# Eighty-four idle transposes ahead of each layer of experts, and two scatters moved behind the counts

## The chip, the cores and the metric

The kernel runs on one core of one Trainium2 chip. The metric is the device time of one execution in microseconds (us); lower is better. A profiled execution was taken by the hardware profiler beside the timed runs. [...] "Cold" below means 0.50, "warm" 1.00.

## The reference

Attention that keeps the 32 largest scores of each row, and then two layers of experts on the 2304 rows of its output. Each row goes to the one expert (of eight) with the highest logit.

```
scores = q @ k.T / 8 ; all but the top 32 of a row are masked ; attn = softmax(scores) @ v
x  = rows of attn                                          # 2304 x 512
# first layer
e  = argmax(x @ w_gate) ; p = softmax(x @ w_gate)[e]
x  = p * (relu(x @ w1[e]) @ w2[e])                          # w1 512x1024, w2 1024x512
# second layer, only for rows with x @ w_skip > 0; the others stay as they are
out = x + p * (relu(x @ w1[e]) @ w2[e])
```

## The kernel before

All matrix products are done in float32 (the products of the experts as three float32r products of a high and a low part). The program has three stages.

The **attention** takes the first 530 us. Each finished tile of 128 rows is gated at once: the expert of each row is picked, its place in that expert's list is counted, and GpSimd (POOL) scatters the row with an indirect DMA into a table in DRAM, `rows[0]`, which is sorted by expert.

The **first layer** of experts (`Moe.layer(0, ...)`, experts g = 0 to 7) reads blocks of 128 rows of one expert after the other. The **second layer** (g = 8 to 15) does the same from `rows[1]`. For one expert, in `Moe.expert`: `xT` transposes each block of rows on TensorE (line 690), ScalarE copies the high part out of PSUM (L692) and VectorE takes the low part (L693); `mm1` makes the hidden units, eight groups of twelve matmuls (L706), whose width (192 to 512 columns) is chosen by the count of rows; `mm2` makes the output, 24 matmuls of 512 columns a block (L730). The first two blocks (j = 0 and 1) are always computed, the others only where the expert has that many rows. The weights come in pieces by DMA into `raw` buffers, and are split into high and low parts by ScalarE (L653) and by GpSimd or VectorE (L655), next to the matmuls.

After each block of the first layer, `FirstPost` gates its rows for the second layer, and its step `places` ends with two scatters on GpSimd's queue (L541): one of the row into `rows[1]`, and one of the row into the kernel's output, which is the final value of a row that skips the second layer. The block is kept meanwhile in one of six buffers `yo`, which `slot(g, j)` picks; expert 7 has its blocks 0 and 1 in `yo2` and `yo3`.

A layer begins in `Moe.layer`: SyncE loads the first blocks of rows (L662, `xg<-x`), which must wait for the scatters into the same table; all engines read the first count of rows into a register (`counts(0)`, L669 and L670); then the experts follow. Between the layers stands a conditional part for experts with more rows than the blocks hold (L803); it isn't entered here, but where its two ways meet GpSimd waits for its own outstanding scatters and then sets their semaphores (`INC_SWDGE_SEM` in the rows) to the count that the other way would have left. A similar conditional part (L1002) stands between attention and the first layer.

At the start of the program the kernel already has idle transposes of the identity matrix, twenty and then six at a time (`keep_warm`, L150), into a PSUM tile that nobody reads.

Of the kernel before, what the change touches and what calls it, by code (L numbers as in the profile page):

```python
# [8 lines left out]
F32 = mybir.dt.float32  # L9
# [467 lines left out]
HF = 5  # L477
D0 = 1
F0 = (0, 1, 2, 3)
LO = ((1, 3, 5, 7), (1, 3, 5))  # L480


# [10 lines left out]
def top_expert(tc, ev, lg, f, ob, mask=None):  # L493


    nc = tc.nc

    def first():
        nc.vector.scalar_tensor_tensor(f[:, 8:16], lg, f[:, 0:1], ev.rev8, op0=OP.is_ge, op1=OP.mult)

    def onehot():
        if mask is None:
            one_port(tc, ev, ob, f[:, 8:16], f[:, 2:3], OP.is_equal)
        else:
            nc.vector.tensor_scalar(ob, f[:, 8:16], f[:, 2:3], mask, op0=OP.is_equal, op1=OP.mult)

    return [lambda: nc.vector.tensor_reduce(out=f[:, 0:1], in_=lg, op=OP.max, axis=AX.X),
            lambda: nc.vector.tensor_scalar(f[:, 1:2], f[:, 0:1], -1.0, None, op0=OP.mult),
            first,
            lambda: nc.vector.tensor_reduce(out=f[:, 2:3], in_=f[:, 8:16], op=OP.max, axis=AX.X),  # L510
            onehot]


def take_place(tc, ev, sb, base, f, ob, r=None):

    nc = tc.nc
    at = []

    def ranks():
        p = ev.ps.tile([128, 2, 8], F32, name="m", bufs=ev.mb)  # L520
        nc.tensor.matmul(p[:, 0], ev.tri, ob, start=True, stop=True)
        nc.tensor.matmul(p[:, 1], ev.ones, ob, start=True, stop=True)
        if r is not None:
            nc.scalar.activation(r, p, AF.Copy)
        at.append(p if r is None else r)

    def move():
        p = at.pop()
        nc.vector.tensor_tensor(f[:, 16:24], p[:, 0], base, op=OP.add)
        nc.vector.tensor_tensor(base, p[:, 1], base, op=OP.add)  # L530

    def pick():
        nc.vector.scalar_tensor_tensor(f[:, 24:32], f[:, 16:24], 1.0, ob, op0=OP.mult, op1=OP.mult,
                                       accum_out=f[:, 3:4])

    return [ranks, move, pick]


def scatter(tc, ev, dst, idx, src, group=None):

    w = tc.nc.gpsimd.indirect_dma_start(out=dst, out_offset=bass.IndirectOffsetOnAxis(ap=idx, axis=0), in_=src,  # L541
                                        in_offset=None, bounds_check=dst.shape[0] - 1, oob_is_err=False)
    if group:
        tc.declare_no_dep(w.ins, group=group, reason="every token has its own row")
        tc.add_to_no_dep_group(group, w.ins)
    return w
# [51 lines left out]
class Moe:  # L598
# [4 lines left out]
    def __init__(self, tc, ev, pool, weights):  # L603
        self.tc, self.ev, self.ws = tc, ev, weights
        self.W1 = [pool.tile([128, 2, 1024], F32R, name="w1_%d" % i) for i in range(4)]
        self.RAW = [pool.tile([128, 1024], F32, name="raw%d" % i) for i in range(3)]
# [26 lines left out]
    def fetch(self, k):  # L633

        if k >= 128:
            return
        layer, e = divmod(k // 8, 8)
        w1, w2 = self.ws[layer]
        raw, c = self.raw(k), k % 8
        if c < 4:  # L640
            self.tc.nc.sync.dma_start(raw, w1[e, c * 128:(c + 1) * 128, :])
        else:
            self.tc.nc.sync.dma_start(raw.rearrange("p (a d) -> p a d", a=2),
                                      w2[e, (c - 4) * 256:(c - 3) * 256, :].rearrange("(a p) d -> p a d", p=128))
# [13 lines left out]
    def load(self, g, j):  # L658
        layer, e = divmod(g, 8)
        rows = self.ev.rows[layer]  # L660
        r0 = e * (rows.shape[0] // 8) + j * 128
        self.tc.nc.sync.dma_start(self.XG[g % 2][j], rows[r0:r0 + 128])  # L662
# [79 lines left out]
    def expert(self, g):  # L742


        layer, e = divmod(g, 8)
        post, nxt = self.posts[layer], e < 7
        for j in range(2):
# [10 lines left out]
        for f in range(8):  # L758
            self.mm1(g, f)
            for i in range(4):  # L760
                if F0[i] == f:
                    self.split(8 * g + 4 + i, post.lo)
# [27 lines left out]
    def layer(self, layer, ns):  # L790
        tc, nc = self.tc, self.tc.nc
        g0 = layer * 8
        self.ns, self.n, self.open_rows = ns, {}, []
        for j in range(BLOCKS[layer]):
            self.load(g0, j)
        self.counts(0)
        if layer == 0:
            for k in range(6, 3 + NR):
                self.fetch(k)
        for e in range(8):  # L800
            self.expert(g0 + e)
        most = nc.values_load(ns[0:1, 8:9], min_val=0, max_val=18)  # L802
        with tc.If(most > BLOCKS[layer]):  # L803
            self.rest(layer, ns)
# [55 lines left out]
def slot(g, j):  # L860
    return j + 2 if j > 1 else 2 * (g % 2) + j


class FirstPost:

    lo = LO[0]

    def __init__(self, tc, ev, mo, wgt, out):
        Dm = out.shape[1]
        self.tc, self.ev, self.out, self.wgt = tc, ev, out, wgt  # L870
        self.yo = [mo.tile([128, Dm + 2], F32, name="yo%d" % i) for i in range(6)]
        self.ix = [mo.tile([128, 2], I32, name="ix%d" % i) for i in range(6)]
        self.fx = [mo.tile([128, 48], F32, name="fx%d" % i) for i in range(6)]
        self.ob = [mo.tile([128, 8], BF, name="ob%d" % i) for i in range(6)]
        self.yT = [mo.tile([128, 4, 128], F32, name="yT%d" % i) for i in range(2)]
        self.rk = [mo.tile([128, 2, 8], F32, name="rk%d" % i) for i in range(6)]
        self.ex = mo.tile([128, 8], F32, name="ex")
        self.D = Dm

    def __call__(self, g, j, xg, p):  # L880
# [4 lines left out]
    def later(self, g, j):  # L885
        tc, nc, ev, D = self.tc, self.tc.nc, self.ev, self.D
        i = slot(g, j)
        y, ix, f, ob, yT = self.yo[i], self.ix[i], self.fx[i], self.ob[i], self.yT[j % 2]
        lg, sk, tok = f[:, 32:40], f[:, 40:41], y[:, D + 1:D + 2]

        def nop():
            pass

        def turn():
            p = ev.ps.tile([128, 4, 128], F32, name="m", bufs=ev.mb)
            for c in range(4):
                nc.tensor.transpose(p[:, c], y[:, c * 128:c * 128 + 128], ev.ident)
            nc.scalar.activation(yT, p, AF.Copy)

        def logits():  # L900
            p = ev.ps.tile([128, 9], F32, name="m", bufs=ev.mb)
            for c in range(4):
                nc.tensor.matmul(p, yT[:, c], self.wgt[:, c], start=(c == 0), stop=(c == 3))
            nc.vector.tensor_copy(f[:, 32:41], p)
            a[0]()
            nc.vector.tensor_scalar(f[:, 41:42], sk, 0.0, None, op0=OP.is_gt)
            a[1]()
            a[2]()
            nc.vector.tensor_scalar(f[:, 42:43], sk, 0.0, OOB, op0=OP.is_le, op1=OP.mult)
            a[3]()  # L910
            nc.scalar.activation(self.ex, lg, AF.Exp, bias=f[:, 1:2], accum_out=f[:, 4:5])
            nc.vector.scalar_tensor_tensor(ix[:, 1:2], f[:, 41:42], OOB, tok, op0=OP.mult, op1=OP.add)
            a[4]()

        def places():
            b[0]()
            nc.vector.tensor_scalar(f[:, 5:6], f[:, 4:5], 1e-9, None, op0=OP.add)
            b[1]()
            nc.vector.reciprocal(y[:, D:D + 1], f[:, 5:6])
            b[2]()  # L920
            nc.vector.tensor_scalar(ix[:, 0:1], f[:, 3:4], f[:, 42:43], None, op0=OP.add)
            scatter(tc, ev, ev.rows[1], ix[:, 0:1], y, ev.moe_groups[0])
            scatter(tc, self.ev, self.out, ix[:, 1:2], y[:, :D], ev.moe_groups[1])

        a = top_expert(tc, ev, lg, f, ob, f[:, 41:42])
        b = take_place(tc, ev, None, ev.base[1], f, ob, self.rk[i])
        return [turn, nop, logits, nop, nop, places]


class SecondPost:  # L930
    lo = LO[1]

# [132 lines left out]
```

## Time and profile before

| | |
|---|---|
| timed runs | 1097.92, 1098.09 and 1105.02 us; median 1098.09 |
| profiled execution, its own time | 1106.61 us |
| its span, first to last instruction | 1104.8 us |
| what lies around the span | 1.8 us |
| granted TensorE clock, mean | 0.914 of full |

The profiled execution is 8.5 us above the median of the runs. Two of the three timed runs are within 0.2 us of one another, the third is 7 us above them. Times inside the profile are counted from the span's start: attention to about 530 us, the first layer to about 865 us, the second to the end.

### The profile page before, as it was taken

The page shows a single profiled execution, that of the slowest core. Times are in us where ns is not written, and L with a number is a line of the kernel's source. Part 1 is how long each engine was busy: PE and PEld are TensorE (multiplying, and loading weights), DVE is VectorE, ACT ScalarE, POOL GpSimd, SP SyncE. Part 2 cuts the span into 40 slices and gives each one's busy share as a digit, 9 for nine tenths or more (in the row PEclk, how much of TensorE's full clock was granted, in tenths as well). Part 3 has the DMA queues.
Part 4 walks back from the last instruction along what each step waited for, and adds up shares of the span by engine and source line. Part 5 has one row for each costly group of instructions (what it writes and reads, how often), then busy time and mean ns, then how long its engine had stood idle before and what let it go on. Part 6 is the DMA issues. An engine that isn't in the chain of part 4 may idle for free. (4 is left out here: it accounts for less than half of the span.)

```text
span 1104.8 us, 20918 instructions
## 1 busy us (share of the span) xinstructions
PE 915.3 (83%) x6389; PEld 725.8 (66%) x6389; DVE 780.9 (71%) x3483; ACT 687.6 (62%) x1420; POOL 621.1 (56%) x451
## 2 busy tenths in 40 slices
PE   7577777787977778789499899988999499999994
PEld 5345554555655455457488778867877398898884
DVE  7999999999899999997226456446635256644441
ACT  5689999997879989975235435435543154443340
POOL 3777887787587978842224344334324266665461
PEclk9689999998888889989599899988999599999998
DMA  9991010101102000001635454456425367665530
GB/s 302 297 265 65 1 65 2 65 2 53 51 33 99 22 20 20 1 2 40 222 116 174 129 151 146 141 167 191 145 88 154 101 187 219 218 211 168 177 103 14
DMA packets 55051, 127.90 MB, mean 116 GB/s; under 512 B 8105, under 2 KB 8105, under 8 KB 54864
## 3 DMA queue, kind: packets, MB, share of 16 engines
q1 hardware_dynamic: 48464, 112.89, 33.1%
q0 software_dynamic: 6400, 12.65, 3.1%
q8 instruction: 101, 1.65, 0.6%
q14 instruction: 86, 0.70, 0.2%
HBM read 96.04 MB, written 37.86 MB: 121 GB/s over the span
## 5 line engine op out<-in xcount | busy, mean ns | idle before, releaser
L655 POOL TENSOR_TENSOR w<-raw,w 128x1024 fp32r<-128x1024 f32 x74 | 179.5, 2435 | 219.4 <-ACT w L653 143.2
L730 PE MATMUL y<-w,h 128*128 128x512 f32 x960 | 240.2, 404 | 10.5 <-ACTq L679 5.0
L212 POOL TENSOR_TENSOR y<-s,sg 128x576 f32<-128x576 f32 x144 | 203.9, 1438 | 64.4 <-ACT sg L209 48.3
L706 PE MATMUL hp<-xT,w 128*128 128x192 f32 (+4 forms) x1536 | 221.1, 302 | 10.7 <-DVE h L721 6.7
L706 PEld LDWEIGHTS hp<-xT,w 128*128 128x128 f32 x1536 | 209.9, 195 | 16.5 <-DVE h L721 8.7
L730 PEld LDWEIGHTS y<-w,h 128*128 128x128 f32 x960 | 181.1, 193 | 54.8 <-issue 10.3
L181 DVE MAX8 ca<-s 128x8 f32<-128x82 f32 (+1 forms) x1008 | 159.3, 228 | 6.1 <-ACT s L170 6.1
L295 PE MATMUL m<-ident,p 128*128 128x128 f32 x576 | 98.0, 298 | 74.4 <-DVE x L326 52.3
L259 POOL TENSOR_TENSOR r<-s,r 128x576 f32<-128x576 f32 x96 | 137.5, 1447 | 28.9 <-DVE r L255 18.4
L295 PEld LDWEIGHTS m<-ident,p 128*128 128x128 f32 x576 | 66.8, 149 | 116.1 <-ACT p L267 31.1
L721 DVE SCALAR_TENSOR_TENSOR h<-hp,h 128x512 fp32r<-128x512 f32 (+1 forms) x128 | 77.8, 621 | 82.6 <-ACT h L720 82.1
L653 ACT ACTIVATE w<-raw 128x1024 fp32r<-128x1024 f32 x128 | 133.6, 1055 | 0.5 <-ACTq L679 0.5
L720 ACT ACTIVATE h<-hp 128x512 fp32r<-128x512 f32 (+1 forms) x128 | 68.3, 543 | 75.2 <-PE hp L706 72.1
L209 ACT ACTIVATE sg<-s,tm 128x576 f32<-128x576 f32 x144 | 111.5, 792 | 5.6 <-POOL tm L200 5.6
L655 DVE TENSOR_TENSOR w<-raw,w 128x1024 fp32r<-128x1024 f32 x54 | 86.9, 1609 | 37.2 <-ACTq L679 27.2
L219 DVE MAX8 my<-y 128x8 f32<-128x576 f32 x144 | 101.9, 746 | 1.9 <-POOL y L212 1.9
L124 PE MATMUL m<-pT,v 128*64 128x128 f32 (+1 forms) x1280 | 95.2, 298 | 8.2 <-ACT pT L301 7.0
L97 PE MATMUL s<-kT,qT 64*128 64x288 f32 x512 | 90.5, 475 | 12.5 <-ACT s L170 12.5
L170 ACT ACTIVATE s<-s 128x1152 f32<-128x1152 f32 (+1 forms) x73 | 81.9, 1123 | 18.8 <-PE s L97 16.2
L301 ACT ACTIVATE pT<-m 128x512 f32<-128x512 f32 x137 | 78.5, 609 | 23.8 <-PE m L295 23.6
L124 PEld LDWEIGHTS m<-pT,v 128*64 128x64 f32 x1280 | 75.3, 155 | 21.4 <-ACT pT L301 11.5
L267 ACT ACTIVATE p<-r,neg 128x576 f32<-128x576 f32 x96 | 74.7, 784 | 3.4 <-POOL r L259 3.2
(133 smaller groups left out, 1302.1 us busy)
## 6 DMA issues: line engine op xcount, KB each, us to landing
raw<-in_moe_w_dram SPq DMA_DIRECT2D x128, 512.0 KB, 4.4
x<-zrow SPq DMA_DIRECT2D x16, 1028.0 KB, 19.2
xg<-x SPq DMA_DIRECT2D x56, 257.0 KB, 3.7
v<-in_v_dram SPq DMA_DIRECT2D x8, 576.0 KB, 4.2
kT<-in_k_dram SPq DMA_DIRECT2D x7, 576.0 KB, 4.4
qT<-in_q_dram SPq DMA_DIRECT2D x7, 576.0 KB, 5.8
out_dram<-yo,ix POOLq DMA_INDIRECT x40, 4.8
kT<-in_k_dram SPq DMA_DIRECT2D x2, 288.0 KB, 3.8
```

The lines of the kernel that those rows point to most:

```text
L97: nc.tensor.matmul(p[:, c, :288], d["qT"][h, b, t * 128:t * 128 + 128], d["kT"][h, b, cs], start=True, stop=True)
L124: nc.tensor.matmul(po[i * 64:i * 64 + 64, cs], d["vt"][:, b, i, c] if c < 4 else d["v8"][i * 64:i * 64 + 64, b], pts[i][:, c, cs] if c < 4 ...
L181: nc.vector.max(out=ca[:, c], in_=e["s"][hh][:, cut[c]:cut[c + 1]])
L209: nc.scalar.activation(sg, e["s"][hh], AF.Sign, bias=bt["tm"][:, w:w + 1], scale=-ONE_BELOW, accum_out=bt["ac"][:, w:w + 1])
L212: nc.gpsimd.tensor_mul(y, e["s"][hh], sg)
L219: nc.vector.max(out=bt["my"][:, 2 * i + hh, 8:], in_=e["y"][hh])
L259: nc.gpsimd.tensor_tensor(r, e["s"][hh], r, op=OP.subtract)
L295: nc.tensor.transpose(pp[:, c], e["p"][:, hh, c * 128:c * 128 + 128], ident)
L653: nc.scalar.activation(t[:, 0], raw, AF.Copy)
L655: eng.tensor_tensor(t[:, 1], raw, t[:, 0].bitcast(F32), op=OP.subtract)
L706: nc.tensor.matmul(p[:, :W], self.w1(g, c)[:, a, fs], x[:, c, b, :W], start=(i == 0), stop=(i == 11))
L730: nc.tensor.matmul(p, self.HT[f][:, a, js], self.W2[f // 2][:, b, f % 2 * 512:f % 2 * 512 + 512], start=(f + a + b == 0), stop=(f == 7 and ...
```

## The change

Two things. In `Moe.layer`, behind the loads of the first rows and the first count, 84 transposes of the identity into a fresh tile `m` of PSUM that nobody reads; so in both layers. And the scatters to the output of blocks 0 and 1 of the first layer's last expert (g = 7) are kept back in a list, and are issued at the beginning of the second layer, behind its `counts(0)`.

```diff
+WARM2 = 84
@@ Moe.layer
         for j in range(BLOCKS[layer]):
             self.load(g0, j)
         self.counts(0)
+        for fn in self.posts[0].skipped:
+            fn()
+        self.posts[0].skipped = []
+        p = self.psum.tile([128, 4, 128], F32, name="m", bufs=self.ev.mb)
+        for i in range(WARM2):
+            nc.tensor.transpose(p[:, i % 4], self.ev.ident, self.ev.ident)
         if layer == 0:
@@ FirstPost.__init__
+        self.skipped = []
@@ FirstPost.later, places()
             scatter(tc, ev, ev.rows[1], ix[:, 0:1], y, ev.moe_groups[0])
-            scatter(tc, self.ev, self.out, ix[:, 1:2], y[:, :D], ev.moe_groups[1])
+            self.skipped.append(lambda: scatter(tc, ev, self.out, ix[:, 1:2], y[:, :D], ev.moe_groups[1]))
+            if g % 8 < 7 or j > 1:
+                self.skipped.pop()()
```

TensorE at the beginning of the first layer, before. `ns` holds the counts, `m` is a tile of PSUM, `xg` a block of rows, `ident` the identity:

```order
L1002 UNCONDITIONAL_BRANCH x2
L669 TENSOR_LOAD ns
L670 TENSOR_LOAD ns
L690 MATMUL m<-ident,xg_10121 128x128 x4
L690 MATMUL m<-ident,xg_10122 128x128 x4
L679 COMPARE_AND_BRANCH x2
L690 MATMUL m<-ident,xg_10124 128x128 x4
L679 UNCONDITIONAL_BRANCH x2
L690 MATMUL m<-ident,xg_10123 128x128 x4
```

The same place after the change (the numbers of the lines are a little higher in the changed file):

```order
L670 TENSOR_LOAD ns
L671 TENSOR_LOAD ns
L803 MATMUL m<-ident 128x128 x84
L691 MATMUL m<-ident,xg_10121 128x128 x4
L691 MATMUL m<-ident,xg_10122 128x128 x4
L680 COMPARE_AND_BRANCH x2
L691 MATMUL m<-ident,xg_10124 128x128 x4
```

The 84 transposes stand between the reading of the counts and the first transposes of rows; nothing else moved on TensorE. At the beginning of the second layer the same 84 stand behind the same two loads of `ns`.

GpSimd at the end of the first layer, before. `yo3` and `yo2` are blocks 1 and 0 of its last expert, `x1` is the table `rows[1]`, `out_0_dram` the output, and L802 and L803 begin the conditional part between the layers:

```order
L541 DMA x1_83<-yo3_10086,ix3_10092 18432x514
L541 DMA out_0_dram<-yo3_10086,ix3_10092 2304x512
L541 DMA x1_83<-yo2_10085,ix2_10091 18432x514
L541 DMA out_0_dram<-yo2_10085,ix2_10091 2304x512
L802 TENSOR_LOAD ns_10157
L803 COMPARE_AND_BRANCH
```

The same place after the change:

```order
L542 DMA x1_83<-yo3_10086,ix3_10092 18432x514
L542 DMA x1_83<-yo2_10085,ix2_10091 18432x514
L809 TENSOR_LOAD ns_10157
L810 COMPARE_AND_BRANCH
```

Only the two scatters to the table are left there. GpSimd after the change where the second layer begins; `ns_17471` holds its counts:

```order
L810 ISA
L810 UNCONDITIONAL_BRANCH
L670 TENSOR_LOAD ns_17471
L542 DMA out_0_dram<-yo3_10086,ix3_10092 2304x512
L542 DMA out_0_dram<-yo2_10085,ix2_10091 2304x512
L680 COMPARE_AND_BRANCH
```

The two scatters to the output moved from between and behind those to the table to the far side of the place where the conditional part ends, and of the reading of the count. The wait for outstanding scatters and `INC_SWDGE_SEM` (the `ISA` row) now stand ahead of them.

## Rows read from the trace of the kernel before

**Rows 1.** The page: busy share of TensorE; granted clock in 40 slices.

```profile
PE 915.3 (83%) x6389; PEld 725.8 (66%) x6389; DVE 780.9 (71%) x3483; ACT 687.6 (62%) x1420; POOL 621.1 (56%) x451
...
PEclk9689999998888889989599899988999599999998
```

**Rows 2.** TensorE's waits over the span: us in total, times, longest us.

```profile
PE m L690 <- DMA xg<-x: 25.3, 3, 12.6
...
PE hp L706 <- DVE h L721: 6.7, 13, 1.0
...
PE y L730 <- ACTq L679: 5.0, 3, 1.7
...
PE m L690 <- DVE xT L693: 4.1, 4, 1.0
```

**Rows 3.** Stretches at the first layer's beginning: us, TensorE busy, clock, DMA share, GB/s.

```profile
525.79:537.79 12.00, 0.00 (x1) 0.50 0.43 143
537.79:543.12 5.33, 3.90 (x16) 0.50 0.89 286
543.12:549.68 6.56, 6.54 (x18) 0.50 1.00 391
549.68:564.88 15.20, 15.20 (x81) 1.00 0.47 145
```

**Rows 4.** The same at the second layer's beginning, and one later `mm1`.

```profile
860.29:876.46 16.17, 2.14 (x13) 0.50 0.23 72
...
879.11:884.19 5.08, 4.91 (x22) 0.50 0.09 33
884.19:892.88 8.69, 8.54 (x76) 1.00 0.53 167
905.16:916.61 11.45, 11.10 (x97) 1.00 0.59 187
```

**Rows 5.** Line 670 at each layer's beginning: ns min/median/max, first and last start.

```profile
L670 PEldq TENSOR_LOAD <-ns x1: 306/306/306, 533.6 to 533.6; - x1
...
L670 PEldq TENSOR_LOAD <-ns x1: 306/306/306, 869.9 to 869.9; - x1
```

**Rows 6.** TensorE's timeline at the program's start: start us, us, instruction, count.

```profile
1.42 4.53 PE L150 MATMUL m<-ident 128*128 128x128 f32 x20 [1.42 <-DVE ident L57]
...
7.57 0.88 PE L150 MATMUL m<-ident 128*128 128x128 f32 x6
```

**Rows 7.** Timeline of `xT` inside the layers, with a warm clock.

```profile
624.57 0.63 PE L690 MATMUL m<-ident,xg 128*128 128x128 f32 x4 [1.02 <-DVE xT L693]
...
901.81 1.03 PE L690 MATMUL m<-ident,xg 128*128 128x128 f32 x8
902.50 1.09 ACT L692 ACTIVATE xT<-m 128x512 fp32r<-128x512 f32 x2 [6.40 <-PE m L690]
...
903.13 1.29 DVE L693 TENSOR_TENSOR xT<-m,xT 128x512 fp32r<-128x512 f32 x2 [2.58 <-ACT xT L692]
```

**Rows 8.** Line 706 alone, 36 matmuls of 416 columns: TensorE and weight loads.

```profile
678.48:685.51 7.03, 7.03 (x36) 6.64 (x36) 1.00 0.66 210
```

**Rows 9.** GpSimd and SyncE between the layers: timelines, and line 803's waits.

```profile
867.65 0.97 POOL L541 DMA_INDIRECT x<-yo,ix  x1 [0.30 <-issue]
868.93 0.97 POOL L541 DMA_INDIRECT out_dram<-yo,ix  x1 [0.30 <-issue]
...
L803 POOLq INC_SWDGE_SEM  x1: 1413/1413/1413, 871.9 to 871.9; - x1
...
873.60 3.26 SPq L662 DMA_DIRECT2D xg<-x  x6
...
884.03 2.39 POOL L655 TENSOR_TENSOR w<-raw,w 128x1024 fp32r<-128x1024 f32 x1 [14.14 <-ACT w L653]
```

**Rows 10.** Line 730 alone, 36 matmuls in two experts of the first layer.

```profile
762.75:774.49 11.74, 11.44 (x36) 8.19 (x36) 0.77 0.53 159
797.86:806.30 8.44, 8.44 (x36) 6.65 (x36) 1.00 0.56 159
```

## The prediction, written before the changed kernel ran

> **What bounds the kernel now.** I read the page first, then TensorE's waits over the whole span, then stretches of some us around the two places that the change touches. TensorE is busy 83% of the span, and from the first layer on nearly without a break; its clock falls to half for one slice at about 530 us and again at about 865 us [rows 1]. Those are the two beginnings of layers. Among its waits the largest one on a DMA is that for the first rows, 25.3 us in three waits, 12.6 the longest [rows 2]. The stretches show what follows: before the first layer TensorE does nothing for 12.0 us, then 5.3 us of transposes and waits at half clock, then 6.6 us of `mm1` at half clock, and only from 549.68 on it has the full one [rows 3]. Before the second layer it is the same with 16.2 us nearly idle and 5.1 us of cold `mm1` [rows 4]. So there is something to gain: 96 matmuls of 416 columns would take 96 x 7.03/36 = 18.7 us warm [rows 8], and took 6.56 + 15.20 = 21.8 [rows 3]; 96 of 192 columns take 11.45 us warm and took 5.08 + 8.69 = 13.8 [rows 4]. That is 3.1 + 2.3 = 5.4 us, and with some 2 us in the cold transposes of rows it is all that a warm clock can give. Behind the two beginnings TensorE sets the end, so what it loses or gains there moves the end by as much.
>
> **When the transposes run.** They stand behind the reading of the counts, line 670 before. In the first layer that load starts at 533.6 and takes 0.3 us, in the second at 869.9 [rows 5]; with the small waits behind it the transposes begin at about 534.0 and 870.3. Neither time hangs on the rows or on the moved scatters. TensorE is idle there, so the first of them are free. The rows let `xT` begin at 537.79 and 876.46 before [rows 3, 4]; what lies behind these points is paid for.
>
> **How long 84 take.** At the program's start the same instruction was cold twenty times: 4.53 us with a tail of 0.42 for the last, so 0.216 each; six later ones took 0.88, and eight transposes of rows inside the second layer 1.03, which with a tail of 0.27 is 0.109 each [rows 6, 7]. How many run cold is not in the trace before, since no such row of transposes stands there. The nearest rows: 5.1 and 6.6 us passed from the first `mm1` matmul to the full clock at the two layers [rows 3, 4], and at the program's start the twenty transposes were cold to the last, while the six that begin at 7.57, 6.2 us after the first of all, were warm [rows 6]. I take 5.5 us, between them. Then 5.5/0.216 = 25 are cold, the other 59 take 6.4 us, and all 84 take 11.9 us. Ends: with 5.1 us cold it is 11.7, with 6.6 it is 12.4. The far ends are 84 x 0.109 = 9.2 us if none were cold, and 84 x 0.216 = 18.1 if all were.
>
> **First layer.** The transposes end at 534.0 + 11.9 = 545.9, so `xT` begins 8.1 us later than before. In return it and `mm1` run warm, and all rows have landed. From the start of `xT` with two blocks the second copy by ScalarE ends 1.8 us later and the second subtraction by VectorE 2.6 us later [rows 7]. Here there are four blocks, and a later block waits for a buffer of PSUM, as the third does with 1.02 us inside the layers [rows 7]; I estimate two more steps of 0.75 us, so the first `mm1` matmul can go at +3.4 and the second, which needs the low part, at +4.1. With 18.7 us of warm matmuls `mm2` begins at about +22.7, so at 568.6. Before it began at 564.88 [rows 3]. The first layer loses 3.7 us.
>
> **Second layer.** The transposes end at 870.3 + 11.9 = 882.2. With two blocks `mm1` is under way at +2.6 [rows 7], and with 11.3 us of warm matmuls (11.45 with its edges, [rows 4]) `mm2` begins at +13.9, so at 896.1; before it was 892.88 [rows 4]. The second layer loses 3.2 us.
>
> **The moved scatters.** Before, the last scatter to the table went out at 867.65 behind one to the output, and another to the output at 868.93 [rows 9]. Then GpSimd waited for all of them to land, set its semaphores for 1.4 us from 871.9, and only when that was done SyncE could load the first rows, at 873.60 [rows 9]. After the change the last scatter to the table takes the place 1.28 us ahead, and no scatter to the output is waited for any more, which lay 1.28 us behind it: the loads can go out 1.3 to 2.6 us earlier, more if setting the semaphores is quicker with fewer scatters open. I take 2.4. But the rows then lie there at about 874 and TensorE is busy with transposes until 882, so this is worth nothing as the change stands; without the transposes it would be worth its 2.4 us. The two scatters themselves come behind GpSimd's reading of the count. What is queued behind them there is the first split of weights, which began at 884.03 after 14.1 us of waiting for ScalarE [rows 9]; two issues of 1.28 us end ten us ahead of that. They share the DMA engines with the rows; a load later by even 2 us is still covered. `yo2` and `yo3` are written again only behind the next expert. The cost is nothing, from none to 0.5 us.
>
> **Sum.** 3.7 + 3.2 = 6.9 us slower; with the ends of 11.7 and 12.4 us for the transposes it is 6.5 to 7.9. Even with every transpose warm, 2.7 us shorter each time, 1.5 us would be lost: the 84 are too many, since they end behind the rows in any case. Against the profile that is 1106.6 + 6.9 = 1113.5. The profile lies 8.5 us above the median of the timed runs, which I take to be other cold stretches than these two, so I put the sum on the median: 1098.1 + 6.9 = 1105.0.
>
> **The rivals.** *Transposes don't wake the clock.* In this case all 84 take 18.1 us, 6.2 more in each layer, and what follows stays cold as before, which costs another 5.4 + 2: 6.9 + 12.4 + 7.4 = 26.7, near 1125, slower by 2.4%. It would decide if the granted clock stays at half through the 84. Against it speaks the program's start, where ahead of the first warm six not much but twenty transposes had run [rows 6]; what ran between, the first matmuls of scores, leaves a rest of doubt. [...]
>
> *Other cold stretches come along.* Inside the first layer the clock also falls where TensorE is only thinned out, not idle: 36 matmuls of `mm2` took 11.74 us with a mean clock of 0.77, against 8.44 in a warm expert, 3.3 us more [rows 10]; that happened in three experts of this execution. Two timed runs are at 1098 and one at 1105, so some executions have about two of them more. If the shifted order, or chance, puts the median of the changed kernel with the slower ones, it is 1105.0 + 6.9 (that is 1105.0 less 1098.1) = 1112, slower by 1.3%. Nothing in the profile says that a shift favours either, and in the runs shown it was one of three.
>
> *The delay is taken up behind (not slower).* TensorE's waits in the layers come to over 15 us: for `h` from VectorE 6.7, for ScalarE ahead of `mm2` 5.0, for `xT` 4.1 [rows 2]. If the engines that it waits for there were paced by the weights and not by TensorE, a TensorE that comes 3.7 us later would find them done, and the 6.9 us would vanish: about 1098, no change. It decides if those waits end on weights. Against it: they repeat with the same size (1.02 us four times, 1.7 three times, by count and longest in [rows 2]), as they do when an engine follows TensorE's own last matmul at a fixed distance.
>
> **How the numbers follow.** The forecast, 1105 (1101 to 1109 with the ends of the cold stretch and a spread of the runs), 0.60. Cold stretches on top, 1112: 0.20. Delay taken up, 1098: 0.13. Transposes that don't wake the clock, 1125: 0.05. The rest, 0.02, for something faster that I don't see. The range leaves out the rule's case and the outer half of the second: 1097 to 1113. A difference under 1% (11 us) is about what a measurement of this kernel can't tell from none: 1109.1 and up is slower by over 1%, which takes the second and fourth case and a little of the first, 0.27; faster by over 1% is 1087 and down, 0.03; within 1% is left with 0.70.
>
> **What would show it.** In the changed profile: 84 transposes from about 534 to 546 and from 870 to 882, the first two dozen at 0.21 us and the rest at 0.11, with a granted clock of 1.00 from about 5.5 us after their start; `xT` that waits for TensorE and not for a DMA; `mm1` of the first expert warm throughout, about 19 us and 11.5; the loads of the second layer's first rows at about 871; `mm2` of the two first experts 3 to 4 us later than before. I am wrong in the main step if the transposes end before the rows land, and wrong in the sum if `mm2` is later by that and the end isn't.

## The result and the profile after

The changed kernel took 1112.06 us (median of 22 runs, 1105.48 to 1118.68), the kernel before 1104.28 (median of 22 runs on the same chip, 1095.83 to 1115.29). The ratio is 1.0075, with a 95% interval of 1.0052 to 1.0097: slower by some 8 us. (The ratios, here and below, are computed from the fast runs of both kernels and not from the medians, so the two can differ by some tenths of a per cent.) The forecast had a loss of 6.9 us on a median of 1098.1. The loss was nearly met, and 1112.06 lies inside the range of 1097 to 1113, near its end. The base was not met: 22 runs put the kernel before at 1104.3, which is near its profiled execution, while the three runs shown earlier lay lower.

The two profiled executions differ by only 4.3 us (spans of 1109.1 and 1104.8), because attention, whose code is the same, happened to be 5.2 us shorter in the one after. So stage times are counted below from the moment at which VectorE finishes making the counts of a layer (L594 before, L595 after). These two rows, one of each kernel, are the starts of that instruction for the first layer, before and after:

```profile
533.13 0.17 DVE L594 TENSOR_SCALAR ns<-ns 128x9 int32<-128x9 int32 x1
```

```profile
527.91 0.17 DVE L595 TENSOR_SCALAR ns<-ns 128x9 int32<-128x9 int32 x1
867.64 0.17 DVE L595 TENSOR_SCALAR ns<-ns 128x9 int32<-128x9 int32 x1
```

For the second layer it was 869.17 before. From the first counts to the end of the span, the layers took 571.7 us before and 581.2 after: 9.5 more, 3.7 in the first layer (336.0 to 339.7) and 5.8 in the second (235.7 to 241.5).

TensorE's timeline at the two beginnings in the changed kernel shows the 84 transposes and what comes behind them:

```profile
528.84 10.68 PE L803 MATMUL m<-ident 128*128 128x128 f32 x84 [8.34 <-DVE ns L595]
539.35 1.47 PE L691 MATMUL m<-ident,xg 128*128 128x128 f32 x12
...
562.01 13.33 PE L731 MATMUL y<-w,h 128*128 128x512 f32 x58
...
868.55 11.47 PE L803 MATMUL m<-ident 128*128 128x128 f32 x84 [6.21 <-PEq L671]
879.86 1.04 PE L691 MATMUL m<-ident,xg 128*128 128x128 f32 x8
...
894.77 9.12 PE L731 MATMUL y<-w,h 128*128 128x512 f32 x39 [1.00 <-PEq L680]
...
920.37 4.84 PE L731 MATMUL y<-w,h 128*128 128x512 f32 x13 [1.99 <-ACT w L654]
```

Neither `xT` (L691) has a wait behind it in brackets: TensorE goes from the last transpose straight to the rows, which lie there. The wait of up to 12.6 us on `xg<-x` [rows 2] is gone, and TensorE's own transposes stand in its place. `xT` begins 11.4 us behind the counts where it was 4.7 (537.79 in [rows 3] less 533.13), and in the second layer 12.2 where it was 7.3 [rows 4].

The same stretches by clock, in the changed kernel (us, TensorE busy, granted TensorE clock as a share of full, share of DMA engines, GB/s). In this profile and in that of the kernel before the clock's records hold 0.50 and 1.00 alone; other values in such rows are means over a stretch:

```profile
528.84:531.55 2.71, 2.71 (x13) 0.50 0.84 252
531.55:539.35 7.80, 7.80 (x73) 1.00 0.98 339
539.35:542.84 3.49, 2.10 (x18) 1.00 1.02 390
542.84:562.01 19.17, 18.90 (x96) 1.00 0.37 115
868.55:872.89 4.34, 4.34 (x21) 0.50 0.06 14
872.89:879.86 6.97, 6.97 (x66) 1.00 0.71 229
879.86:894.77 14.91, 12.49 (x107) 1.00 0.37 109
```

The clock goes to 1.00 after 2.7 and 4.3 us of transposes and stays there through `xT` and `mm1`. That answers to the cold `mm1` of [rows 3] and [rows 4]: 19.2 us where it was 6.56 + 15.20. So the warm clock came, and was worth what was thought; but it was bought with transposes that end later than the rows arrive. Behind the counts, `mm2` of the first expert begins at 34.1 us (before 31.7) and 27.1 (before 23.7): 2.4 and 3.4 us lost there.

### The profile page after: what moved, and what is told of

It is laid out like the page before. It is cut to its first block, busy times and chain, and to the rows that moved or that the text cites. A ratio compares the mean times of both kernels' runs of the same rounds, so it can differ in the third digit from the quotient of the medians.

```text
span 1109.1 us, 21259 instructions
## 1 busy us (share of the span) xinstructions
PE 924.4 (83%) x6557; PEld 737.6 (67%) x6557; DVE 786.0 (71%) x3483; ACT 686.8 (62%) x1420; POOL 621.7 (56%) x451
## 3 DMA queue, kind: packets, MB, share of 16 engines
q8 instruction: 103, 1.69, 0.6%
## 5 line engine op out<-in xcount | busy, mean ns | idle before, releaser
L707 PE MATMUL hp<-xT,w 128*128 128x192 f32 (+4 forms) x1536 | 216.8, 299 | 11.0 <-DVE h L722 8.7
L707 PEld LDWEIGHTS hp<-xT,w 128*128 128x128 f32 x1536 | 206.2, 192 | 15.7 <-DVE h L722 10.8
L656 DVE TENSOR_TENSOR w<-raw,w 128x1024 fp32r<-128x1024 f32 x54 | 95.0, 1759 | 37.9 <-ACTq L680 27.9
L97 PE MATMUL s<-kT,qT 64*128 64x288 f32 x512 | 85.7, 454 | 12.5 <-ACT s L170 12.5
L693 ACT ACTIVATE xT<-m 128x512 fp32r<-128x512 f32 x40 | 21.8, 596 | 98.5 <-PE m L691 96.5
```

What stands on the lines that cost most here:

```text
L97: nc.tensor.matmul(p[:, c, :288], d["qT"][h, b, t * 128:t * 128 + 128], d["kT"][h, b, cs], start=True, stop=True)
L656: eng.tensor_tensor(t[:, 1], raw, t[:, 0].bitcast(F32), op=OP.subtract)
L707: nc.tensor.matmul(p[:, :W], self.w1(g, c)[:, a, fs], x[:, c, b, :W], start=(i == 0), stop=(i == 11))
```

## The experiments

Two questions were open. Is the loss only the length of the 84 transposes, so that fewer, or earlier ones, turn it into a gain? And what is the rest of the second layer's loss, which shows behind the first `mm2` as waits of TensorE that were not there before: the moved scatters, or the transposes? The edits below are to the changed kernel, or to the kernel of the experiment whose lines they remove. Single runs are told beside the kernel before on the same chip.

**The scatters alone** (`scatters_only`): the transposes are left out.

```diff
-        p = self.psum.tile([128, 4, 128], F32, name="m", bufs=self.ev.mb)
-        for i in range(WARM2):
-            nc.tensor.transpose(p[:, i % 4], self.ev.ident, self.ev.ident)
```

> Only the two scatters are moved; no transposes. Measured from the instruction that makes the counts to the first mm2 matmul (31.75 us in the first layer and 23.71 in the second before; 34.10 and 27.13 with the whole change). My theory: first layer 31.7 as before; in the second the rows are loaded 2.4 us earlier, and with nothing to hide it mm2 comes 2.4 us earlier, so 21.3. Rival A (the moved scatters disturb GpSimd or the DMA engines, and so cost the two new stalls of TensorE in the second layer, 1.00 us before the first expert's mm2 and 1.99 us before the second expert's): the stalls are here too, and the second layer gains little. Rival B (the stalls come with the 84 instructions in TensorE's stream): no such stalls here.

One run took 1108.16 us (before: 1105.07, median of 23). SyncE's load of the second layer's first rows and TensorE's `xT`, from the timelines, then the stretches up to `mm2`:

```profile
868.61 3.25 SPq L663 DMA_DIRECT2D xg<-x  x6
871.60 1.94 PE L691 MATMUL m<-ident,xg 128*128 128x128 f32 x8 [10.73 <-DMA xg<-x]
```

```profile
871.60:881.57 9.97, 9.08 (x40) 0.50 0.32 108
881.57:889.10 7.53, 7.38 (x67) 1.00 0.66 195
```

The counts are made at 866.1 here, so the loads go out 2.5 us behind them, where it was 4.4 before: 1.9 us earlier, near the 2.4 of the prediction. But `mm2` begins at 23.0 behind the counts, only 0.7 earlier than the 23.7 before. The clock rises 15.5 us behind the counts, and it was 15.0 before (884.19 in [rows 4]); rows that come sooner are worked on at half clock for longer. So even without transposes the earlier load isn't worth its 2.4 us, as the prediction said it would be, but 0.7.

Behind `xT` TensorE has no wait of a microsecond in the first two experts of this layer. But the layers took 575.4 us, 3.8 more than before, although `mm2` came earlier in both: 5.4 us were lost behind the second layer's first `mm2`. TensorE's branches of line 714, which it meets once a group of `mm1`, show where (ns min, median and max, first and last start), and so does its clock around the longest of them:

```profile
L714 PEldq COMPARE_BRANCH  x7: 208/208/4533, 955.0 to 964.4; - x7
```

```profile
958.99:963.48 4.49, 2.92 (x24) 1.00 0.93 314
963.48:970.31 6.83, 5.54 (x18) 0.50 0.56 204
```

One branch took 4.5 us, TensorE stood for 2.71 us, and the clock was at half for 6.8 us. A late branch with a cold stretch behind it comes without any transposes, too.

**The transposes alone** (`transposes_only`): the scatters go back to their old place.

```diff
-            self.skipped.append(lambda: scatter(tc, ev, self.out, ...))
-            if g % 8 < 7 or j > 1:
-                self.skipped.pop()()
+            scatter(tc, self.ev, self.out, ix[:, 1:2], y[:, :D], ev.moe_groups[1])
```

> Only the 84 transposes a layer; the scatters stay where they were. My theory: the row loads go out 4.4 us after the counts as before instead of earlier, but the transposes cover that, so counts to mm2 is 34 us in the first layer and 27 in the second, as with the whole change. Rival A (the stalls of 1.00 and 1.99 us in the second layer come of the moved scatters): 24 to 26 in the second layer, and no such stalls. Rival B (they come with TensorE's stream of instructions, which is the same as with the whole change): the same two stalls at the same two places.

One run took 1117.70 us (before: 1105.07). The layers took 583.3 us, 2.1 more than with both parts of the change, and `mm2` begins 35.1 and 26.0 us behind the counts. TensorE's timeline in the second layer:

```profile
876.07 11.05 PE L803 MATMUL m<-ident 128*128 128x128 f32 x84 [6.57 <-PEq L671]
...
901.03 9.13 PE L731 MATMUL y<-w,h 128*128 128x512 f32 x39 [0.15 <-ACT w L654]
...
927.45 4.78 PE L731 MATMUL y<-w,h 128*128 128x512 f32 x13 [2.83 <-ACT w L654]
```

The transposes alone bring a loss as large as that of the whole change. Of the two waits in the second layer the one ahead of the first expert's `mm2` is gone (0.15 us where it was 1.00); the one ahead of the second expert's is here too, 2.83 us where it was 1.99 with both parts. So the moved scatters aren't needed for it.

**Twice as many transposes** (`twice`), which asks whether a delay at the beginning is taken up behind.

```diff
-WARM2 = 84
+WARM2 = 168
```

> The whole change with 168 transposes a layer in place of 84. My theory (each transpose behind the landing of the rows is paid in full): the other 84 are all warm, 84 x 0.109 = 9.2 us a layer, so counts to mm2 goes from 34.1 and 27.1 us to 43.3 and 36.3. Rival (a later TensorE is made up for by waits behind, so part of the delay vanishes before the layer's end): the first layer as a whole grows by clearly less than 9 us from the 339.7 us with the change.

One run took 1128.11 us (before: 1100.57). TensorE's timeline:

```profile
529.47 21.00 PE L803 MATMUL m<-ident 128*128 128x128 f32 x168 [8.35 <-DVE ns L595]
550.30 1.47 PE L691 MATMUL m<-ident,xg 128*128 128x128 f32 x12
...
879.00 20.33 PE L803 MATMUL m<-ident 128*128 128x128 f32 x168 [6.43 <-PEq L671]
```

Beside the kernel before, `mm2` begins 14.2 us later in the first layer (46.0 behind the counts against 31.7) and 12.3 later in the second (36.0 against 23.7), 26.5 together; the layers take 597.8 us against 571.7, 26.1 more. The first layer was expected at 43.3: the clock rose later than with 84 (5.1 us after the first transpose and not 2.7) and fell once more, for 3.4 us, just behind `xT`. A late beginning isn't given back, and the rival of the delay that is taken up falls. That the two sums agree to 0.4 us is closer than a pair of profiles can show: what lies behind the first `mm2` of a layer differs by 5 to 6 us among these kernels.

**Ten plain matmuls in place of the 84 transposes** (`ten_matmuls`), ten of 512 columns with the identity (the trace records each as two), of nearly the same total time. If transposes woke the clock later or not at all, these would do it sooner.

```diff
-WARM2 = 84
+WARM2 = 10
-        p = self.psum.tile([128, 4, 128], F32, name="m", bufs=self.ev.mb)
+        p = self.psum.tile([128, 512], F32, name="m", bufs=self.ev.mb)
-            nc.tensor.transpose(p[:, i % 4], self.ev.ident, self.ev.ident)
+            nc.tensor.matmul(p, self.ev.ident, self.ev.zrow[:, :512], start=True, stop=True)
```

> The whole change, but in each layer 10 plain float32 matmuls of the identity with 512 columns of zeros instead of the 84 transposes; they keep TensorE busy for about as long (10 to 12 us) in a tenth of the instructions. If transposes count for the clock as matmuls do, the full clock comes 2.7 to 5.6 us after the start of the ten, as with transposes, and counts to mm2 is 33 to 35 and 25 to 27 us. If transposes count for less, it comes clearly earlier than 2.7 us. If the stalls of 1.0 to 2.8 us that all kernels with transposes show in front of mm2 in the second layer come of where the instructions lie in TensorE's stream, they are at other places than with 84; if they come of a warm or late first expert, they are at the same place.

One run took 1103.15 us (before: 1100.57). The cold stretch and the warm one behind it, in the first layer and in the second:

```profile
525.21:530.24 5.03, 5.00 (x6) 0.50 0.90 257
530.24:536.38 6.14, 6.14 (x16) 1.00 1.02 380
864.49:868.17 3.68, 3.68 (x5) 0.50 0.26 71
868.17:874.97 6.80, 6.80 (x18) 1.00 0.58 202
```

The clock rises 5.0 and 3.7 us after the first matmul, and 5.1 and 6.1 in `early_matmuls` below; after the first transpose it took between 2.7 and 5.9 us in eight kernels (2.7 and 4.3 with the change, 4.6 and 3.5 with the transposes alone, 5.1 and 3.7 with twice as many; the others, below, lie between 2.8 and 5.9). No difference of kind. `mm2` begins at 36.2 (33 to 35 were expected) and 25.8, no better than with the transposes; in the first layer a cold stretch of 3.4 us came just behind the thin `xT`, at the beginning of `mm1`. TensorE's waits ahead of and inside the second layer's first two `mm2` stay below half a microsecond here.

**Transposes that end with the rows** (`fitted`): 30 in the first layer and 16 in the second.

```diff
-WARM2 = 84
+WARM2 = (30, 16)
-        for i in range(WARM2):
+        for i in range(WARM2[layer]):
```

> The whole change with 30 transposes in the first layer and 16 in the second, at the same place, so that they end about when the rows land. My theory (what is lost is the time by which the transposes outlast the rows): 30 take about 6 us, 16 about 3.5; counts to mm2 29 us in the first layer (2.6 less than before) and 19 in the second (4.8 less); 7 us faster than before, ratio 0.993. Rival (the transposes cost by being there, through the stalls and the added instructions): no faster than before, and stalls of 1 to 2 us in the second layer.

The median of 12 runs is 1099.63 us against 1105.07: a ratio of 0.9945, 0.9917 to 0.9974. In the first layer 30 transposes take 6.35 us, `xT` starts without a wait, and `mm2` begins 29.9 us behind the counts, 1.9 earlier than before. Nearly all of the thirty were cold; no other kernel's transposes took longer to the full clock:

```profile
526.22:532.14 5.92, 5.92 (x28) 0.50 0.87 281
```

The second layer missed its expectation by 5 us. Its stretches:

```profile
862.85:866.65 3.80, 3.65 (x16) 0.50 0.01 1
866.65:870.06 3.41, 1.26 (x8) 1.00 0.97 307
870.06:876.89 6.83, 6.09 (x27) 0.50 0.28 92
876.89:885.98 9.09, 7.94 (x72) 1.00 0.60 179
```

The sixteen end at 866.50 and the rows come at 868.61. The clock rises just behind the last transpose, and 3.4 us later, with TensorE busy 1.26 of them, it is down again for 6.8 us. `mm2` begins at 24.1: what was won is lost, most of it in the gap. The stalls that the rival named came as well, 1.15 us ahead of the first expert's `mm2`, behind a branch of 3.1 us, and 1.64 ahead of the second's; the kernel was faster all the same.

**Transposes ahead of the counts** (`early`): 40 and 25, put in front of `counts(0)`, so that TensorE begins them without waiting for VectorE.

```diff
-WARM2 = 84
+WARM2 = (40, 25)
+        p = self.psum.tile([128, 4, 128], F32, name="m", bufs=self.ev.mb)
+        for i in range(WARM2[layer]):
+            nc.tensor.transpose(p[:, i % 4], self.ev.ident, self.ev.ident)
         self.counts(0)
...
```

> The whole change, but the transposes stand ahead of the reading of the counts and not behind it, 40 in the first layer and 25 in the second: TensorE waits for the counts idly, for 3 us in the first layer and 1 us in the second. My theory: the clock is up by the time that the rows land and nothing outlasts them: counts to mm2 28.6 us in the first layer (3.1 less than before) and 18.3 in the second (5.4 less); 8.5 us faster than before, ratio 0.992. Rival (idle transposes gain nothing that a cold mm1 doesn't give back elsewhere, for example in waits for weights): ratio 1.000, with new waits of TensorE in the first expert's mm2.

The median of 12 runs is 1100.64 us against 1105.07: 0.9952, 0.9919 to 0.9986. `mm2` begins at 29.9 and 22.1. The stretches of the first layer's beginning:

```profile
528.06:533.19 5.13, 5.13 (x24) 0.50 0.14 28
533.19:540.01 6.82, 4.05 (x34) 1.00 0.84 274
540.01:543.43 3.42, 3.26 (x8) 0.50 1.05 419
```

The transposes ended 0.23 us before the first two blocks of rows; then `xT` waited 1.78 us for the next two, and the clock fell for 3.4 us. In the second layer a wait of 1.11 us for the rows was followed by 6.8 us at half clock, and `mm2` came 3.8 us later than expected.

**The same, longer** (`early_longer`): 52 and 42 ahead of the counts, so that no gap is left.

```diff
-WARM2 = (40, 25)
+WARM2 = (52, 42)
```

> The transposes ahead of the counts, as before with 40 and 25, but 52 and 42, so that they end when the rows have landed and not 0.2 to 1.1 us ahead of that. With 40 and 25 the clock came up at 2.7 and 4.0 us behind the counts and fell again 6.8 and 3.4 us later, because xT then waits for rows. My theory: without that gap the clock stays up; counts to mm2 28.5 us in the first layer and 20 in the second (29.9 and 22.1 with 40 and 25); against the kernel before ratio 0.992. Rival (the clock falls in the thin xT whatever stands ahead of it): no shorter than 29.9 and 22.1, and a clock of 0.5 within 10 us behind the counts.

The median of 12 runs is 1098.45 us against 1100.57: 0.9967, 0.9933 to 1.0000. The first layer from the first transpose to `mm2`:

```profile
523.54:528.66 5.12, 5.12 (x24) 0.50 0.38 116
528.66:554.40 25.74, 24.09 (x142) 1.00 0.71 247
```

That is the clean case: 5.1 us cold where TensorE would have been idle, then the full clock throughout, and `mm2` 28.5 us behind the counts, 3.3 earlier than before. In the second layer the clock stayed up through `xT` and most of `mm1`, but `mm2` began at 24.4, where 20 was expected. The stretches there, TensorE's timeline at the last group of `mm1`, and its branches of line 714:

```profile
857.44:863.17 5.73, 5.73 (x27) 0.50 0.08 25
863.17:880.24 17.07, 13.75 (x111) 1.00 0.57 189
880.24:887.07 6.83, 6.68 (x22) 0.50 0.61 177
```

```profile
879.95 2.64 PE L707 MATMUL hp<-xT,w 128*128 128x192 f32 x12 [1.81 <-DVE h L722]
```

```profile
L714 PEldq COMPARE_BRANCH  x13: 208/208/3633, 868.1 to 879.7; - x13
```

One branch took 3.6 us instead of 0.2, inside the first expert's `mm1`; TensorE waited 1.81 us there, half of what the layer should have gained, and the clock fell right behind it, so that the last group of `mm1` and the first half of `mm2` ran cold.

**The same without the moved scatters** (`early_longer_back`): `early_longer` with the plain scatter of `transposes_only`.

> The same with the two scatters back where they stood before the change. My theory: the rows of the second layer are loaded 4.4 us behind the counts and not 2.5 to 4, so xT begins at about 7.3 us and mm2 1 to 2 us later than with the scatters moved; in the whole that is not to be told from it (ratio 0.993). Rival (moving the scatters gains nothing, since the landing of the last scatter to the table decides): the same time to mm2 as with them moved.

The median of 12 runs is 1100.36 us against 1100.57: 0.9990, 0.9955 to 1.0025. `mm2` begins at 28.3 and 24.6. The loads of the second layer's rows go out 4.2 us behind the counts, so `xT` waits 1.84 us for them and the clock falls for 6.8 us. But `mm2` is only 0.2 us later than with the scatters moved, where 1 to 2 were expected. As `early_longer` lost 1.8 us and more to its late branch, the two don't show what the earlier load is worth here; nor do the times, whose intervals overlap.

**Plain matmuls ahead of the counts** (`early_matmuls`): seven and six of 512 columns in place of the 52 and 42 transposes.

```diff
-WARM2 = (52, 42)
+WARM2 = (7, 6)
-            nc.tensor.transpose(p[:, i % 4], self.ev.ident, self.ev.ident)
+            nc.tensor.matmul(p, self.ev.ident, self.ev.zrow[:, :512], start=True, stop=True)
```

> As with 52 and 42 transposes ahead of the counts, but 7 plain float32 matmuls of 512 columns in the first layer and 6 in the second in their place, which end at about the same time (6 us behind the counts) in a seventh of the instructions. If the stalls of TensorE in the second layer (1.81 us in the first expert's mm1 with 52 and 42) come of the added instructions: no stall over 1 us in the first two experts, counts to mm2 28.5 and 19.5 to 22 us, ratio to before 0.992. If not: stalls as with 52 and 42 and 24 us in the second layer, ratio 0.996.

The median of 12 runs is 1101.30 us against 1106.05: 0.9987, 0.9950 to 1.0024. TensorE's timeline of the second layer:

```profile
865.44 8.41 PE L799 MATMUL m<-zrow,ident 128*128 128x512 f32 x12 [4.37 <-DVEq L810]
873.69 1.04 PE L691 MATMUL m<-ident,xg 128*128 128x128 f32 x8
...
887.75 4.59 PE L731 MATMUL y<-w,h 128*128 128x512 f32 x19
```

`mm2` begins at 28.8 and 21.5 us behind the counts: the earliest of all in the second layer, 2.3 ahead of the kernel before. No wait of a microsecond stands in its first two experts, so this is what a second layer's beginning gains when no branch is late there. The whole kernel is not shown to be faster for it: the interval reaches over 1.

**The first layer alone** (`first_only`): 52 transposes ahead of the counts, none in the second layer, with the scatters moved.

```diff
-WARM2 = (52, 42)
+WARM2 = (52, 0)
+        if layer == 0:
...
```

> 52 transposes ahead of the counts in the first layer, none in the second, and the scatters moved. Counts to mm2 28.4 us in the first layer as with 52 and 42. In the second layer the two theories: if transposes gain there, mm2 comes later than with any of them that end with the rows, that is over 24.4 us; if they gain nothing there, 23.0 as with the scatters moved alone. Ratio to before 0.993 to 0.997.

The median of 12 runs is 1099.75 us against 1106.05: 0.9978, 0.9944 to 1.0011. `mm2` begins at 28.7 and 22.5. So of the two theories the second came out: with no idle work in the second layer its `mm2` is as early as with `early`'s 25 transposes (22.1) and earlier than with `fitted`'s 16 and `early_longer`'s 42 (24.1 and 24.4). Only the six matmuls did clearly better there (21.5). The loads went out 2.3 us behind the counts here, 2.2 earlier than before, and `mm2` is 1.2 earlier than before.

All of them together; `mm2` is counted from the making of the counts, and the layers from the first counts to the end of the span:

| kernel | idle work, first / second layer | `mm2`, us | layers, us | ratio to before |
|---|---|---|---|---|
| before | none | 31.7 / 23.7 | 571.7 | |
| the change | 84 / 84 behind the counts | 34.1 / 27.1 | 581.2 | 1.0075 |
| `scatters_only` | none | 31.3 / 23.0 | 575.4 | one run |
| `transposes_only` | 84 / 84 | 35.1 / 26.0 | 583.3 | one run |
| `twice` | 168 / 168 | 46.0 / 36.0 | 597.8 | one run |
| `ten_matmuls` | 10 / 10 matmuls | 36.2 / 25.8 | 577.0 | one run |
| `fitted` | 30 / 16 | 29.9 / 24.1 | 573.0 | 0.9945 |
| `early` | 40 / 25 ahead of them | 29.9 / 22.1 | 568.1 | 0.9952 |
| `early_longer` | 52 / 42 ahead | 28.5 / 24.4 | 570.7 | 0.9967 |
| `early_longer_back` | 52 / 42 ahead | 28.3 / 24.6 | 568.1 | 0.9990 |
| `early_matmuls` | 7 / 6 matmuls ahead | 28.8 / 21.5 | 569.2 | 0.9987 |
| `first_only` | 52 / none, ahead | 28.7 / 22.5 | 567.7 | 0.9978 |

The six kernels whose idle work is cut to the wait for the rows, more or less, start their first `mm2` 1.8 to 3.5 us earlier than before. A gain of that size is at the edge of what these runs tell; two of them, `fitted` and `early`, have an interval that ends below 1, and they beat the kernel before by half a per cent. Which of the six is best isn't shown. Their own medians lie within 3 us, while that of the kernel before, taken anew beside each group, moved by 5.5 (1100.6 to 1106.1). And the order of the ratios isn't that of the gains at `mm2`: `early_matmuls` gained most there, 5.2 us in both layers, and has 0.9987; `fitted` gained least, 1.5, and has 0.9945.

## Why the prediction was right, and where it was off

**The main step held.** The prediction said that 84 transposes outlast the rows and that TensorE sets the end behind them. The change shows the first (`xT` with no wait ahead of it), `twice` shows the second (26.5 us late at the two `mm2`, 26.1 at the end), and `fitted` and `early` show the converse: with shorter ones the loss is gone and a small gain stands in its place. That the total came out so near, 6.9 us against some 8, is partly luck: at the two `mm2` the change lost 5.8 us, and the rest arose behind them, in stretches that differ as much among kernels without regard to the idle work.

**How long 84 take.** Predicted 11.9 us, measured 10.5 and 11.3 from their start to that of `xT`. The rate per transpose was right (0.21 us cold and 0.11 warm: 2.71 us with 13 of them and 7.80 with 73 in the first layer; that the twenty at the program's start were cold was read from 0.21 us each, since the clock's records begin at 6.96 us there); the cold stretch was mis-sized, 5.5 us where it was 2.7 and 4.3. Over all kernels with transposes that stretch runs from 2.7 to 5.9 us, and eleven of the fifteen are shorter than the lower end of the range, 5.1.

**First layer.** Predicted 3.7 us lost at `mm2`, measured 2.4; the cold stretch is 2.8 us shorter, which saves 25 - 13 = 12 transposes at half of 0.216 us, or 1.3 us. From `xT` to `mm2` the prediction had 22.7 us, and it took 22.66. By the layer's end the loss was 3.7; the 1.3 us more arose between the first `mm2` and the second counts, where the kernels of this study differ by 6 us among themselves (301.3 to 307.3 us), with no pattern that follows the idle work.

**Second layer.** Predicted 3.2 us lost at `mm2`, measured 3.4, but not for the reason given: the transposes were 0.6 us shorter than said, and from `xT` to `mm2` it took 14.9 us in place of 13.9, since a wait of 1.00 us came in. Line 680 is a branch on the count of rows. The first row below is TensorE's branches there in the changed kernel, in the 7 us around that wait, the second the same place in the kernel before (ns min, median and max, first and last start):

```profile
L680 PEldq COMPARE_BRANCH  x2: 208/1593/2978, 891.6 to 894.8; - x2
```

```profile
L679 PEldq COMPARE_BRANCH  x2: 208/208/208, 890.6 to 892.9; - x2
```

A branch that took 0.2 us before took 3.0. Then came 1.99 us ahead of the second expert's `mm2` and a stretch of 3.4 us at half clock right behind it. The term that the prediction lacked is this: 2.4 us behind the first `mm2`. The wait of 1.99 us is put down to ScalarE's split of `w`. ScalarE's timeline has that piece, and the last `h` behind it:

```profile
917.46 1.05 ACT L654 ACTIVATE w<-raw 128x1024 fp32r<-128x1024 f32 x1
918.41 0.49 ACT L721 ACTIVATE h<-hp 128x384 fp32r<-128x384 f32 x1
```

It ended at 918.5, 1.9 us ahead of the `mm2` that is said to wait for it; ScalarE wasn't late. The wait is in `transposes_only` too (2.83 us), and `fitted` and `early` have one of 1.64 and 1.40 us at the same place; with the scatters alone, with `twice` and with ten matmuls there is none of a microsecond. Late branches are in each of the nine kernels whose branches were read over both layers, the one before among them: the longest took 2.1 us in `transposes_only`, 2.7 before, 3.0 with the change and 4.5 in `scatters_only`, and they stand at places that differ.

What comes just ahead of these waits can be read from the DMA queues. One of them, `q8 instruction` in the profile, carried 103 packets of 16 KB in the changed kernel (1.69 MB). Its rows there from 892.0 to 893.2, inside the branch of 3.0 us, and from 918.0 to 919.2, ahead of the wait of 1.99 (packets, MB, share of the 16 engines):

```profile
q8 instruction: 1, 0.02, 4.9%
```

```profile
q8 instruction: 1, 0.02, 4.9%
```

The first of these packets lands at 893.15, 1.4 us before the branch ends at 894.59; the second at 919.10, 1.3 us before `mm2` goes on at 920.37. In the profiles of the kernel before and of the change together, 11 branches of lines 680 and 714 (679 and 713 before) take more than a microsecond, and each of them ends 1.36 to 1.64 us behind the landing of such a packet; of the 863 short ones 42, or 5%, end so far behind one. That TensorE waits there for instructions which are still being loaded would fit these times, but no row names what releases a branch: it is a guess and isn't shown. From 535 us to the end 72 such packets come in the kernel before and 74 with the change; whether the added instructions decide which branches are late isn't shown either.

**The moved scatters.** Worth nothing, as predicted, and for the reason predicted: in the changed kernel TensorE is busy until 879.9 and the rows are there before. But the loads go out only 0.3 us earlier than before (4.10 us behind the counts against 4.43), where 2.4 was predicted, and 1.9 earlier without the transposes. GpSimd waited longer for its scatters to the table: 5.0 us to landing against 3.4. Over the kernels with moved scatters the loads go out 2.3 to 4.1 us behind the counts, and 2.7 in `early`, which has transposes; so the transposes don't decide it, and why it varies is open.

**The rivals.** *Transposes don't wake the clock* is refuted: the granted clock is 1.00 after 2.7 and 4.3 us of nothing but transposes, and ten plain matmuls do it no sooner (5.0 and 3.7). The runs show this for transposes of 128 x 128 in float32 (`nc.tensor.transpose`, MATMUL in the rows); the case of 1125, which the range left out, didn't come. *The delay is taken up behind* falls with `twice`. *Other cold stretches come along* is partly what happened in the second layer (the 3.4 us behind its second expert's wait), and its price is at most half of those 3.4, 1.7 us of the 8 measured. That 1112 is the number given for this rival is chance: the base had moved, not the loss.

**The base.** The prediction put the 8.5 us between the profiled execution and the median down to cold stretches in the first layer. That was wrong. The same three cold stretches stand in the changed kernel's first layer, at 603, 723 and 760 us. What differs most between executions is attention: its last counts are made anywhere from 524.3 to 536.8 us in the twelve profiles, all with the same code there, and the profile shown ahead of the prediction had 533.1. With 22 runs the median before is 1104.3.

## What to carry to other kernels

In these runs idle work that brought TensorE's clock up paid only as far as it lay inside a wait: begin it as early as TensorE is free (ahead of the wait for a register, not behind it: `mm2` of the first layer at 28.5 us with `early_longer` and not 29.9 with `fitted`) and end it when the data lands. Too long was paid for in full, some 0.11 us for each warm transpose (7.80 us with 73 of them in the changed kernel; the layers took 26.1 us more with `twice`); with too short a row the clock fell again (`early`: a wait of 1.78 us, then 3.4 us at half clock). So measure the wait in each place and size each by itself. An earlier load was worth little where what it feeds ran at half clock: 1.9 us earlier gave 0.7 at `mm2` (`scatters_only`), and 2.2 gave 1.2 (`first_only`).

## What the runs showed of the hardware that was not expected

- **The rise of the clock varies.** After the first of a row of uninterrupted transposes it took from 2.7 us (the change, first layer) to 5.9 (`fitted`, first layer) until the granted clock was 1.00.
- **Short gaps were followed by longer stretches at half clock.** In `fitted` the wait of 2.11 us and the thin `xT` behind it were followed by 6.8 us at half clock; in `early` a wait of 1.78 us by 3.4. So were two late branches: that of 4.5 us in `scatters_only` and that of 3.6 us in `early_longer`, each by 6.8 us at half clock.
- **Branches of TensorE.** Those of lines 680 and 714 take 0.2 us in the median; but the longest of a profile took 2.1 to 4.5 in the nine that were read over both layers, mostly at another place, and in the kernel before and the changed one each of the 11 that took over a microsecond ends 1.36 to 1.64 us behind the landing of a 16 KB packet of the queue `q8 instruction`.
- **Attention varies by 12.5 us** between executions of identical code, with a mean clock up to 525 us between 0.88 and 0.91 in the six profiles where it was read (0.90 in the kernel before, 0.91 in the changed one).

So a faster or slower stage outside the change can hide a change of this size in a pair of profiles; only the count from a common event, or many runs, shows it.
